# Two channels to a weight load in the last four table builds of a fused linear-attention and state-space kernel

## The chip, the cores and the metric

The kernel runs on one core of one Trainium2 chip. The metric is the device time of one execution in microseconds. The core has five engines that run side by side and wait for each other by semaphores: TensorE (PE, matmuls, and PEld, its weight loads), VectorE (DVE), ScalarE (ACT), GpSimd (POOL) and SyncE (SP). SP, POOL and ACT also issue DMAs, each in the order of its own queue. Matmul results land in PSUM and are copied out ("evicted") by ACT or DVE.

## The reference

Two independent parts share one output of 2048 rows and 896 columns.

Part A is a linear attention with 16 heads of 28 channels. Queries and keys go through a 28x28 matrix per head and become features by softmax of the plus and of the minus value; the output is `phi_q (phi_k^T v) / (phi_q sum(phi_k) + 1e-6)`, followed by the output projection.

Part B is a long convolution over 2048 positions for each of 448 channels. Its kernel is a sum over 256 complex states:

```python
P = jnp.exp(logdA[:, :, None] * l[None, None, :])
K = jnp.einsum("dn,dnl,dn->dl", Cc, P, dB).real
...
Yf = Uf * Kf[None, :, :, :]
```

with `logdA = dt * (A_re + i A_im)`. The convolution is done by Fourier transform in the reference; `u * Dskip` is added.

## The kernel before, in words

**Part B's table.** The position l is split into a high part (32 values, list `HI`) and a low part (50 values, list `LO`). For each state, `exp(logdA * l)` is the product of a high power, times C and B, and a low power. So K for one channel is a 32 x 50 table: the matrix product of the high rows (tile `U`, 256 states x 32) with the low rows (tile `W`, 256 states x 50), over real and imaginary parts. The 448 channels are done in eight groups k = 0 to 7 of 56 channels. The 256 states are two halves of 128, which lie on the partitions.

For each group there are five steps:
- `dampings` (L687) makes the damping factors by Exp on ACT, `rotations` (L692) the cosines and sines by Sin on ACT, both out of PSUM.
- `hi_tables` (L714) makes the high rows from powers of the step: four levels with a product of 1792 elements and then sums, differences or the pair step, and two levels (the fourth and the sixth) in which a DMA on POOL's queue adds to what is there. A copy of the first four rows comes by DMA, and two small copies with signs (`SN`) by ACT or DVE.
- `damp` (L700) multiplies rotations by dampings on DVE in two products (step damp) and negates a part on ACT or DVE (step neg, L712).
- `build_k` (L761) forms the tables: in two halves of seven channels from each of four quarters, 112 matmuls a half, each with a weight load of 32 columns (one channel's high rows) and 50 moving columns (its low rows). Channels of the four quarters use the four 32-column strips of the array side by side; four matmuls accumulate (two state halves, real and imaginary). Each half is evicted, 350 columns, into `Ts`.
- `scatter_k` (L903) moves the tables by many small DMAs into `Kt`, ordered by position. It exists once for groups 0 to 3 (sc0), once for 4 and 5 (sc1), once for 6 and 7 (sc2), 48 DMAs each.

Then `kernel_spectrum` (steps ks0, ks1, ks2) multiplies `Kt` with Fourier tables on PE, `signal_spectrum` (us) does the same for the signal, `conv_group` (conv0 to conv2) multiplies the two spectra on DVE, `inverse` (inv) goes back on PE, and the result is written. The products of conv2 need the tables of groups 6 and 7.

**Part A** is woven in: `key_pair` (key, kn), `query` (qe, qz, q), with Exp on ACT, products at L878 and L349 on DVE.

**Order.** Each operation is recorded as a unit by a helper (`tt` L349, `act` L362, `copy` L372, `mm` L382, `dma` L397), and nothing is issued at once. The list `ORDER` names every unit with its engine (P, V, A, G, S for PE, DVE, ACT, POOL, SP), and `PLACES` names the PSUM buffer kind of each PSUM tile. `Plan.run` issues the units in this order; each engine works through its own part of the list and stops at the first instruction whose inputs are not there. Both lists were written by a planner outside the kernel. Some units may go to either ACT or DVE (evictions, sign copies, negations); the list decides.

Of the kernel before, what the change touches and what calls it, by code (L numbers as in the profile page):

```python
# [9 lines left out]
BF16 = mybir.dt.bfloat16  # L10
# [53 lines left out]
def _dft_tables():  # L64
# [27 lines left out]
    for hh in range(4):  # L92
# [3 lines left out]
ORDER = ("23G 26P 39P 0A 48A 29P 24P 3S 1S 2S 4S 17G 8G 34P 27P 44P 43P 13S 192S 47P 49V 52V 51V 53V 50V 54P 55V 56P 57A "  # L96
# [200 lines left out]
def kernel(  # L297
# [134 lines left out]
    Wr = sb("W", [128, 2, N_LO, 2, COLS], BF16, oW)  # L432
    W = Wr.rearrange("p k l c x -> p k c l x")
    E = sb("E", [128, 2, N_LO - 1, COLS], BF16, oE)
    U = sb("U", [128, 2, N_HI, 2, COLS], BF16, oU)
    Kt = sb("Kt", [128, N_KT, D_MODEL], BF16, 0)


# [721 lines left out]
```

## Time and profile before

| | |
|---|---|
| median of 3 runs | 290.28 us (289.6 to 291.36) |
| the profiled execution | 289.75 us |
| its span, first to last instruction | 287.9 us |
| mean granted TensorE clock | 0.992 |
| PE, PEld busy | 253.1, 202.6 us |
| DVE busy | 268.4 us (360 instructions) |
| ACT busy | 239.3 us (537 instructions) |
| POOL busy | 82.8 us |

Times in the profile are microseconds from the start of the span. A group of instructions is given with its line, engine, operation, shapes and count, then the busy time and the mean duration in ns, then the time the engine was idle just before them and what ended that. Instructions on one engine overlap a little, so durations are longer than the distance from start to start. Helpers give their line to all that is recorded through them: L349 are all products and sums on DVE, L362 the functions on ACT, L372 evictions, L382 matmuls, L397 DMAs.

### The profile page before, as it was taken

The page shows a single profiled execution, that of the slowest core. Times are in us where ns is not written, and L with a number is a line of the kernel's source. Part 1 is how long each engine was busy: PE and PEld are TensorE (multiplying, and loading weights), DVE is VectorE, ACT ScalarE, POOL GpSimd, SP SyncE. Part 2 cuts the span into 40 slices and gives each one's busy share as a digit, 9 for nine tenths or more (in the row PEclk, how much of TensorE's full clock was granted, in tenths as well). Part 3 has the DMA queues.
Part 4 walks back from the last instruction along what each step waited for, and adds up shares of the span by engine and source line. Part 5 has one row for each costly group of instructions (what it writes and reads, how often), then busy time and mean ns, then how long its engine had stood idle before and what let it go on. Part 6 is the DMA issues. An engine that isn't in the chain of part 4 may idle for free.

```text
span 287.9 us, 10151 instructions
## 1 busy us (share of the span) xinstructions
PE 253.1 (88%) x4280; PEld 202.6 (70%) x4280; DVE 268.4 (93%) x360; ACT 239.3 (83%) x537; POOL 82.8 (29%) x133
## 2 busy tenths in 40 slices
PE   7895798989978989979888889999899798999993
PEld 3454347668944778957755777769889687989983
DVE  2999997999999999999999999999999989799990
ACT  2999989999999999999999999999996162473241
POOL 2011024050604002030198232468250299000000
PEclk9999899999999999999999999999999999999999
DMA  6996333181546115142064255269969669786033
GB/s 186 298 268 179 71 96 82 24 207 27 84 81 138 32 29 107 34 100 61 11 116 70 56 113 141 54 112 293 238 137 287 224 163 242 222 270 227 18 128 130
DMA packets 41678, 38.54 MB, mean 134 GB/s; under 512 B 21168, under 2 KB 39000, under 8 KB 41506
## 3 DMA queue, kind: packets, MB, share of 16 engines
q1 hardware_dynamic: 33701, 30.14, 36.2%
q0 software_dynamic: 6480, 7.72, 14.9%
q8 instruction: 33, 0.54, 0.8%
q10 hardware_dynamic: 1453, 0.05, 0.3%
q14 instruction: 11, 0.09, 0.1%
HBM read 23.99 MB, written 7.34 MB: 109 GB/s over the span
## 4 chain that ended last, share of the span: by engine, by line
ACT 38%; DVE 23%; PE 14%; DMA 13%; issue 8%; SPq 2%; ACTq 1%; POOL 0%; DVEq 0%; POOLq 0%
ACT sbuf L362 29%; DVE sbuf L349 19%; PE mm L382 7%; ACT sbuf L372 6%; DMA sbuf<-sbuf 5%; PE kb L382 4%; DMA SUd<-sbuf 3%; SPq L397 2%; ACT L362 2%; DVE sbuf L372 2%; PE arg L382 2%; DMA sbuf<-in_B_u_dram 2%; DMA sbuf<-SUd 2%; DMA sbuf<-in_B_A_re_dram 1%; DVE sbuf L353 1%
## 5 line engine op out<-in xcount | busy, mean ns | idle before, releaser
L382 PEld LDWEIGHTS <-sbuf 128*32 128x32 bf16 (+4 forms) x4056 | 190.5, 119 | 72.5 <-issue 39.1
L349 DVE TENSOR_TENSOR sbuf<-sbuf 128x448 bf16<-128x448 bf16 (+9 forms) x213 | 205.3, 1007 | 2.6 <-ACT sbuf L372 1.8
L382 PE MATMUL mm<-sbuf 128*32 128x50 bf16 (+9 forms) x2676 | 157.0, 262 | 18.7 <-ACT sbuf L372 11.1
L362 ACT ACTIVATE sbuf<-arg 128x224 bf16<-128x224 f32 (+5 forms) x312 | 136.8, 676 | 0.1
L397 POOL DMA_DIRECT2D sbuf<-sbuf x99 | 65.0, 762 | 106.5 <-DVE sbuf L349 44.7
L372 ACT CAST sbuf<-mm 128x448 bf16<-128x448 f32 (+3 forms) x90 | 56.5, 657 | 21.5 <-PE mm L382 19.7
L382 PE MATMUL kb<-sbuf 128*32 128x50 bf16 (+10 forms) x790 | 64.6, 250 | 5.6 <-issue 2.0
L382 PE MATMUL arg<-sbuf 128*128 128x112 bf16 (+4 forms) x590 | 44.6, 225 | 1.4 <-ACT sbuf L362 1.2
L372 ACT CAST sbuf<-kb 128x448 bf16<-128x448 f32 (+4 forms) x42 | 24.2, 611 | 12.7 <-PE kb L382 11.0
L397 POOL DMA_DIRECT2D SUd<-sbuf x18 | 14.3, 827 | 45.4 <-ACT sbuf L372 35.9
L362 ACT ACTIVATE sbuf<-mm 112x512 bf16<-112x512 f32 x38 | 24.9, 798 | 0.0
L878 DVE TENSOR_TENSOR sbuf<-arg,sbuf 128x896 bf16<-128x896 f32 x16 | 17.3, 1085 | 1.3 <-PE kb L382 0.6
L362 ACT ACTIVATE sbuf<-sbuf 128x896 f32<-128x896 f32 (+3 forms) x13 | 13.0, 1038 | 1.8 <-DMA sbuf<-in_B_log_dt_dram 1.8
L362 ACT ACT_TABLE_LOAD x10 | 12.8, 1283 | 1.4 <-PEq L1144 1.2
L372 DVE CAST sbuf<-mm 128x448 bf16<-128x448 f32 (+2 forms) x17 | 10.1, 592 | 0.4 <-PE mm L382 0.3
L349 DVE TENSOR_TENSOR sbuf<-mm,sbuf 128x896 bf16<-128x896 bf16 (+1 forms) x17 | 9.3, 554 | 0.0
L812 PE MATMUL mm<-sbuf 112*128 112x112 bf16 x112 | 7.8, 212 | 1.7 <-DVE sbuf L807 0.9
L812 PEld LDWEIGHTS <-sbuf 112*128 112x128 bf16 x128 | 7.3, 97 | 2.7 <-issue 2.4
L372 DVE COPY sbuf<-kb 112x512 bf16<-112x512 bf16 (+1 forms) x18 | 7.2, 406 | 1.5 <-PE kb L584 1.5
L584 PEld LDWEIGHTS <-sbuf 128*112 128x112 bf16 x64 | 5.3, 129 | 3.9 <-issue 3.0
L584 PE MATMUL kb<-sbuf 128*112 128x128 bf16 x64 | 6.1, 219 | 2.2 <-DVE sbuf L372 1.3
L372 ACT CAST sbuf<-arg 128x224 bf16<-128x224 f32 (+1 forms) x10 | 3.5, 373 | 5.0 <-PE arg L382 5.0
(39 smaller groups left out, 69.9 us busy)
## 6 DMA issues: line engine op xcount, KB each, us to landing
sbuf<-const SPq DMA_DIRECT2D x37, 224.0 KB
sbuf<-sbuf POOLq DMA_DIRECT2D x21, 224.0 KB, 4.1
sbuf<-const SPq DMA_DIRECT2D x6, 512.0 KB
sbuf<-in_B_u_dram SPq DMA_DIRECT2D x6, 448.0 KB
sbuf<-in_A_x_dram SPq DMA_DIRECT2D x4, 448.0 KB
out_dram<-sbuf SPq DMA_DIRECT2D x16, 112.0 KB
sbuf<-SUd SPq DMA_DIRECT2D x1, 1792.0 KB
sbuf<-SUd SPq DMA_DIRECT2D x2, 896.0 KB
```

Source lines behind the costliest of these rows:

```text
L349: lambda: nc.vector.tensor_tensor(out=at(out_), in0=at(a), in1=at(b), op=op), [whose(a), whose(b)], [out_])
L353: lambda: nc.vector.scalar_tensor_tensor(out=at(out_), in0=at(a), scalar=sc, in1=at(b), op0=op0, op1=op1),
L362: lambda: nc.scalar.activation(at(out_), at(a), func, scale=scale, bias=bias),
L372: lambda e: (nc.scalar.copy if e == "ACT" else nc.vector.tensor_copy)(at(out_), at(a)), [whose(a)], [out_])
L382: nc.tensor.matmul(out_, lhsT=lhsT, rhs=rhs, start=start, stop=stop, **kw)
L397: plan.add({e: own[e] for e in engs}, lambda e=engs[0]: QUEUES[e].dma_start(out=out_, in_=in_, **kw), r, w, lat=lat, load=pieces / 16000 * ...
L584: mms(p, [lambda t, j=j, x=x: nc.tensor.transpose(t[:, j, :], x[:, 112 * j:112 * j + 112], ident[:, :]) for j in range(4)], 0.4, [x, ident ...
L812: mms(pt, [lambda t, i=i, s=s, c=c: nc.tensor.transpose(t[:, s, 112 * c:112 * c + 112], EKT[:, s, c, 128 * i:128 * i + 128], id112) for s ...
L878: nc.vector.tensor_tensor(out=heads, in0=num(pn.t), op=ALU.mult, in1=SC[:, t4].unsqueeze(3).to_broadcast([128, 2, 16, D_HEAD]))
```

## The change

- In groups 4 to 7 the build takes two channels at once: a weight load of 64 columns (the high rows of two channels) and 100 moving columns (the low rows of both). Of the four 32 x 50 products that come out, the two in which both sides are of the same channel are used. Two such matmuls lie side by side in the two 64-column halves of the array. A group takes 112 matmuls instead of 224, in three PSUM tiles of 5, 5 and 4 channel columns (40, 40 and 32 matmuls), evicted with 500, 500 and 400 columns.
- For that the high rows are kept as two halves of 56 columns (`US`), and `hi_split` takes the place of `hi_tables` in these groups: each product of 1792 elements becomes two of 896, the pair step's two operations become four, the first copy two DMAs.
- `Ts` of groups 4 to 7 holds both columns of products, so it is twice as large and lies elsewhere; `scatter_k` reads the half that belongs to a channel. The order of channels within the states changes for all groups (`states`).
- `ORDER` and `PLACES` are new throughout: 1601 units instead of 1565.

```diff
-        return t.rearrange("p (c n g q) -> p n c g q", c=NCHK, n=2, g=4)
+        return t.rearrange("p (c g n q) -> p n c g q", c=NCHK, n=2, g=4)
...
+    def hi_split(k, rank):
+        step(f"hi{k}.0", rank)
+        cols = slice(k * COLS, (k + 1) * COLS)
+        u = US[:, k % 2]
...
+        for v in range(2):
+            dma(["SP", "POOL"], u[:, v, 0:4].rearrange("p n r x -> p (n r) x"), split(H[:, :, :, cols])[:, v],
+                r=[H[:, :, :, cols]], w=[u[:, v, 0:4]])
+
+        def times(j, src):
+
+            t2 = sb("t2", [128, 2, 2, 4, 2, CW], BF16, oT2)
+            for i in range(2):
...
+                tt(t2[:, i], a, power(j, i).unsqueeze(2).to_broadcast([128, 2, 8, CW]), ALU.mult)
+            return t2
...
+                dma(["POOL"], dst, t2[:, :, :, :, :], r=[t2[:, :, :, :, :], dst], w=[dst], lat=6, cost=0.85, accum_op=ALU.add)
...
+                for v in range(2):
+                    tt(pair(v, 9, 15), a[:, v, ::-1], b[:, v], ALU.subtract)
+                    tt(pair(v, 8, 17), a[:, v], b[:, v, ::-1], ALU.add)
...
-    def build_k(k, Ts, x0, rank):
-        for hq in range(2):
-            step(f"build{k}.{hq}", rank)
+    def build(k, Ts, x0, rank):
+        wide = k > 3
+        for part, (q0, nq) in enumerate(((0, 5), (5, 5), (10, 4)) if wide else ((0, 7), (7, 7))):
+            step(f"build{k}.{part}", rank)
             p = ps(("mm", "kb"), [128, 512])
             calls = []
-            for qq in range(7):
-                q = 7 * hq + qq
+            for qq in range(nq):
                 for i in range(4):
                     nch, ri = i // 2, i % 2
-                    for g in range(4):
-                        xc = nch * CW + g * NQ + q
-                        calls.append(lambda t, g=g, qq=qq, i=i, ri=ri, xc=xc: mm(
-                            t[32 * g:32 * g + 32, qq * N_LO:(qq + 1) * N_LO], U[:, k % 2, :, ri, xc],
-                            W[:, k % 2, ri, :, xc], i == 0, i == 3, tile_position=(0, 32 * g)))
...
+                    for g in range(2):
+                        xc = 28 * g + NQ * nch + q0 + qq
+                        if wide:
+                            calls.append(lambda t, g=g, qq=qq, i=i, ri=ri, xc=xc: mm(
+                                t[64 * g:64 * g + 64, qq * 2 * N_LO:(qq + 1) * 2 * N_LO].rearrange("p (v l) -> p v l", v=2),
+                                US[:, k % 2, :, :, ri, xc].rearrange("p v h -> p (v h)"),
+                                W[:, k % 2, ri, :, xc:xc + CW + 1:CW].rearrange("p l v -> p v l"),
+                                i == 0, i == 3, tile_position=(0, 64 * g)))
+                            continue
...
+            if wide:
+                copy(Ts[:, :, :, x0 + q0:x0 + q0 + nq],
+                     (p, lambda t, nq=nq: t[:, 0:2 * N_LO * nq].rearrange("p (c v l) -> p v l c", c=nq, v=2)))
...
-                    v = Ts[32 * g + h0:32 * g + h1, l0:l1:s, :]
+                    p1 = 64 * (g % 2) + 32 * (g // 2)
+                    v = (Ts[:, g // 2] if gi else Ts)[p1 + h0:p1 + h1, l0:l1:s, :]
...
-        hi_tables(k, 1020 + 100 * k)
+        (hi_split if k > 3 else hi_tables)(k, 1020 + 100 * k)
```

More of the change, by code (lines that the diff above doesn't have):

```diff
@@ L94, in _dft_tables @@
     return tuple(_round_bf16(t) for t in (G, GI, FT, pid, hm))
-ORDER = ("23G 26P 39P 0A 48A 29P 24P 3S 1S 2S 4S 17G 8G 34P 27P 44P 43P 13S 192S 47P 49V 52V 51V 53V 50V 54P 55V 56P 57A "
[75 rows of a table removed]
-PLACES = ("kmmkmmmmkmkmmkmkkmmkmkkmmkmkmkmmmammkkmkkmkmkmkmkkkkmkmmkmkkmmmmkkkmmkmmkaakkmmakakmmkmakkmkmkmkmmkmmkmmmmamaamm"
-         "ammmammmmmmmmmmmmmmmamammammmmmmmmamamaamammmmammmmammmmmmammammmmmmmmmmkamkakaamkkammkakakkmkmmakmakammkkmkmamk"
-         "kammkmkmkkmammkmkkaammakmkmkmkkmamkmkamkmaammkmmkkmmamkmakmmkmmkkmmaammmakmkmkmmma")
+ORDER = ("17G 23G 33P 35P 42P 27P 31P 0A 48A 44P 26P 40P 34P 2S 1S 6S 49V 50V 53V 51V 52V 56P 57V 54P 84P 85V 55A 67A 3S "
[77 rows of a table added]
+PLACES = ("kmmkkkkkmmmkkmmkkkkmkmkmkmkkmmkkkmmmkkmmkmkamkmkmkkmkkmkkkmkmmkkmmkmkmkmkmkkammamkakmmkmakmmkmmkmmmkkmmammamamma"
+         "mmmmammmmmmmmmmmmammammmammammmmmammmmaamammammmmmmmmammmaammammmmmamkkkamkmaakamakkmmkmkaakmmakkmmmmkaakmkmkakk"
+         "kmmmmakkkamkkmmmkkmamkaakmmkmkkmakmkmamkkkmmmakmkakmmmkkakmkmmakmkammkmamammkmaakmmmkk")
 ENGINES = {"P": "PE", "V": "DVE", "A": "ACT", "G": "POOL", "S": "SP"}
@@ L406 @@
     SN = sb("SN", [128, 2, COLS], BF16, oPID + 3584)
+    SNS = sb("SNS", [128, 2, 2, CW], BF16, oPID + 3584)
     H = sb("H", [128, 4, 2, NCOL], BF16, oH)
@@ L435 @@
     U = sb("U", [128, 2, N_HI, 2, COLS], BF16, oU)
+    US = sb("US", [128, 2, 2, N_HI, 2, CW], BF16, oU)
     Kt = sb("Kt", [128, N_KT, D_MODEL], BF16, 0)
@@ L759, in hi_tables, with split, power, pair @@
                 tt(dst[:, :, 1], t2[:, 0, :, 1], t2[:, 1, :, 0], ALU.add)
-    def build_k(k, Ts, x0, rank):
-        for hq in range(2):
-            step(f"build{k}.{hq}", rank)
+    def hi_split(k, rank):
+        step(f"hi{k}.0", rank)
+        cols = slice(k * COLS, (k + 1) * COLS)
+        u = US[:, k % 2]
+        def split(t):
+            return t.rearrange("p n r (v x) -> p v (n r) x", v=2)
+        def power(j, i):
+            return PW[j][:, i, cols].rearrange("p (v x) -> p v x", v=2)
+        for v in range(2):
[4 more added lines that the diff above has]
+            for i in range(2):
+                if src is H:
+                    a = split(src[:, :, :, cols])
+                else:
+                    a = src.rearrange("p v n r x -> p v n (r x)")
+                tt(t2[:, i], a, power(j, i).unsqueeze(2).to_broadcast([128, 2, 8, CW]), ALU.mult)
+            return t2
+        step(f"sn{k}", rank)
+        sine = power(512, 1)
+        for r, f in enumerate((1.0, -1.0)):
+            plan.add({"ACT": 0.15, "DVE": 0.11}, lambda e, r=r, f=f: nc.scalar.mul(SNS[:, :, r, :], sine, f) if e == "ACT" else
+                     nc.vector.tensor_scalar_mul(SNS[:, :, r, :], sine, f), [sine], [SNS[:, :, r, :]])
+        for lv, (j, dst, src, tmp) in enumerate(((256, u[:, :, 8:12], H, None), (128, None, u[:, :, 8:12], None),
+                                                 (512, u[:, :, 16:20], u[:, :, 0:16:4], None),
+                                                 (512, u[:, :, 20:24], u[:, :, 2:16:4], 3584),
+                                                 (512, u[:, :, 24:28], u[:, :, 16:20], None),
+                                                 (512, u[:, :, 28:32], u[:, :, 24:28], 5376))):
+            step(f"hi{k}.{lv + 1}", rank)
+            if tmp:
+                t2 = sb("tm", [128, 2, 4, 2, CW], BF16, oT2 + tmp)
+                tt(t2[:, :, :, ::-1, :], src.rearrange("p v n r x -> p v n (r x)"),
+                   SNS.rearrange("p v r x -> p v (r x)").unsqueeze(2).to_broadcast([128, 2, 4, COLS]), ALU.mult)
+                tt(dst, src.rearrange("p v n r x -> p v n (r x)"),
+                   power(512, 0).unsqueeze(2).to_broadcast([128, 2, 8, CW]), ALU.mult)
+                dma(["POOL"], dst, t2[:, :, :, :, :], r=[t2[:, :, :, :, :], dst], w=[dst], lat=6, cost=0.85, accum_op=ALU.add)
+                continue
+            t2 = times(j, src)
+            if dst is None:
+                uf = u.rearrange("p v n r x -> p v (n r) x")
+                a, b = (t2[:, i].rearrange("p v n r x -> p v r n x") for i in range(2))
+                def pair(v, first, gap):
+                    w = uf[:, v, first:first + gap + 7]
+                    return bass.AP(tensor=w.tensor, offset=w.offset, ap=[w.ap[0], [gap * CW, 2], [2 * CW, 4], [1, CW]])
+                for v in range(2):
+                    tt(pair(v, 9, 15), a[:, v, ::-1], b[:, v], ALU.subtract)
+                    tt(pair(v, 8, 17), a[:, v], b[:, v, ::-1], ALU.add)
+                tt(uf[:, :, 8:16], uf[:, :, 8:16],
+                   BACK[:, cols].rearrange("p (v x) -> p v x", v=2).unsqueeze(2).to_broadcast([128, 2, 8, CW]), ALU.mult)
+            else:
+                tt(dst[:, :, :, 0], t2[:, 0, :, :, 0], t2[:, 1, :, :, 1], ALU.subtract)
+                tt(dst[:, :, :, 1], t2[:, 0, :, :, 1], t2[:, 1, :, :, 0], ALU.add)
@@ L775, in build_k @@
-            mms(p, calls, 2.9, [U[:, k % 2], W[:, k % 2]], mode=1, act=4800)
-            copy(Ts[:, :, x0 + 7 * hq:x0 + 7 * hq + 7],
-                  (p, lambda t: t[:, 0:7 * N_LO].rearrange("p (c l) -> p l c", c=7)))
+                    for g in range(2):
[6 more added lines that the diff above has]
+                                i == 0, i == 3, tile_position=(0, 64 * g)))
+                            continue
+                        for v in range(2):
+                            calls.append(lambda t, g=g, qq=qq, i=i, ri=ri, xc=xc, v=v: mm(
+                                t[64 * g + 32 * v:64 * g + 32 * v + 32, qq * N_LO:(qq + 1) * N_LO], U[:, k % 2, :, ri, CW * v + xc],
+                                W[:, k % 2, ri, :, CW * v + xc], i == 0, i == 3, tile_position=(0, 64 * g + 32 * v)))
@@ new lines, in build @@
+            mms(p, calls, 0.0265 * len(calls) if wide else 2.9, [U[:, k % 2], W[:, k % 2]], mode=1,
+                act=100 * len(calls) if wide else 4800)
+            if wide:
+                copy(Ts[:, :, :, x0 + q0:x0 + q0 + nq],
+                     (p, lambda t, nq=nq: t[:, 0:2 * N_LO * nq].rearrange("p (c v l) -> p v l c", c=nq, v=2)))
+            else:
+                copy(Ts[:, :, x0 + q0:x0 + q0 + nq],
+                     (p, lambda t: t[:, 0:7 * N_LO].rearrange("p (c l) -> p l c", c=7)))
@@ L1067, in table @@
         gi = (0, 0, 0, 0, 1, 1, 2, 2)[k]
-        if k in (0, 4, 6):
-            tss[gi] = sb("Ts", [128, N_LO, 28 * GROUPS[gi][1]], BF16, oTs + (2744 if gi == 2 else 0))
+        if k == 0:
+            tss[0] = sb("Ts", [128, N_LO, 56], BF16, oTs)
+        elif k in (4, 6):
+            tss[gi] = sb("Ts", [128, 2, N_LO, 28], BF16, (oV - 96, oTs)[gi - 1])
         damp(k, 1000 + 100 * k)
-        build_k(k, tss[gi], NQ * (k - (0, 4, 6)[gi]), 1000 + 100 * k)
+        build(k, tss[gi], NQ * (k - (0, 4, 6)[gi]), 1000 + 100 * k)
     def chunk(k, exps, rots):
```

152 rows, old and new, of the table ORDER are left out of this document.

## The prediction

> **What bounds the kernel now.** I read the busy time and the 40 slices first, then the busy time of each engine in single stretches, then the groups by shape, the chain that ended last, and the timeline of DVE.
>
> ```profile
> PE 253.1 (88%) x4280; PEld 202.6 (70%) x4280; DVE 268.4 (93%) x360; ACT 239.3 (83%) x537; POOL 82.8 (29%) x133
> DVE  2999997999999999999999999999999989799990
> ACT  2999989999999999999999999999996162473241
> ...
> 160.00:185.00 25.00, 22.60 (x609) 19.08 (x608) 24.66 (x37) 24.97 (x61) 7.20 (x11) 1.00 0.41 96
> 213.00:233.00 20.00, 17.46 (x384) 15.49 (x382) 19.37 (x13) 10.95 (x22) 4.55 (x9) 1.00 0.77 238
> 251.00:280.00 29.00, 27.86 (x463) 26.67 (x461) 28.23 (x28) 12.90 (x31) 0.00 (x0) 1.00 0.50 163
> ```
>
> A stretch shows its length, then busy us (and instructions) of PE, PEld, DVE, ACT, POOL. Up to 213 us DVE and ACT are both full: 24.66 and 24.97 of 25 us. From 213 us ACT has room (10.95 of 20), and DVE stays near full to 280 us (28.23 of the last 29). PE is never the fullest engine before 213 us, though its share (22.6 of 25) includes waits inside pipelined matmuls. So two engines bound the first three quarters, and DVE, fed by PE, the last.
>
> ```profile
> L382 PE MATMUL mm<-sbuf 128*32 128x50 bf16 x1568 | 38.7, 269 | 2.5 <-issue 2.0 <-ACT sbuf L372 0.4
> L349 DVE TENSOR_TENSOR sbuf<-sbuf 128x1792 bf16<-128x1792 bf16 x47 | 50.2, 1077 | 0.0
> L349 DVE TENSOR_TENSOR sbuf<-sbuf 128x448 bf16<-128x448 bf16 x48 | 16.6, 377 | 0.0
> L372 ACT CAST sbuf<-mm 128x350 bf16<-128x350 f32 x9 | 6.3, 704 | 2.1 <-PE mm L382 2.1
> L712 ACT ACTIVATE sbuf<-sbuf 128x1680 bf16<-128x1680 bf16 x4 | 7.2, 1803 | 0.0
> ...
> 125.63 0.38 DVE L349 TENSOR_TENSOR sbuf<-sbuf 128x448 bf16<-128x448 bf16 x1
> 125.93 0.61 DVE L372 CAST sbuf<-mm 128x448 bf16<-128x448 f32 x1
> 126.46 1.08 DVE L349 TENSOR_TENSOR sbuf<-sbuf 128x1792 bf16<-128x1792 bf16 x1
> 127.46 0.61 DVE L349 TENSOR_TENSOR sbuf<-mm,sbuf 128x896 bf16<-128x896 bf16 x1
> 128.00 0.61 DVE L349 TENSOR_TENSOR sbuf<-sbuf 128x896 bf16<-128x896 bf16 x1
> ```
>
> The build matmuls take 38.7/1568 = 24.7 ns of PE each, so one group (224) some 5.5 us. On a full engine an instruction costs its start-to-start time, not its duration: the timeline gives 1.00 us for 1792 elements, 0.54 for 896, 0.30 for 448, and 0.53 for an eviction of 448. On ACT, back-to-back starts give 0.42 us for a 448-column eviction, 0.48 for 512, 0.36 for the strided 350, 1.50 for the negation at L712, 0.14 for 112 columns.
>
> ```profile
> 215.30 4.11 DVE L349 TENSOR_TENSOR sbuf<-sbuf 128x7616 bf16<-128x7616 bf16 x1
> 279.88 0.61 DVE L349 TENSOR_TENSOR sbuf<-sbuf 128x896 bf16<-128x896 bf16 x1
> ...
> 220.41 2.67 PE mm L382 x100
> 223.09 1.28 PE kb L382 x51
> 224.37 1.95 issue
> 226.32 1.51 PE kb L382 x49
> ```
>
> The end hangs on group 7: its damping (damp7) leaves DVE at 219.3, its build runs on PE from 220.4 to 227.8 with a gap of 1.95, then come eviction, scatter, the last spectra and the last DVE product, done at 280.5. DVE works nearly all of those 61.2 us: its instructions there sum to 57.5 by starts, which leaves 3.7 us of waits.
>
> **Builds, PE.** 896 pairs of 32-column load and 50-column matmul (896 x 24.7 ns = 22.1 us) become 448 pairs of 64 and 100. No row shows such a pair. Lower bound: the same 24.7 ns, as if each pair cost its issue alone; upper bound: the untiled 128x112 matmul, 20.8 us/380 = 54.7 ns, scaled to 100 columns, 49 ns. The tiled builds are the nearer row; I take 28 ns, 12.5 us. PE is relieved of 9.6 us (bounds 0.1 and 11.0), 2.4 us a group. For groups 4 to 6 the time is hidden behind full DVE and ACT and counts nothing; if that cover were gone it would be up to 7.2 us. For group 7 it shortens the build in the chain, but DVE has other work meanwhile: nothing again.
> The row says a 50-column matmul costs about 25 ns. [...]
>
> **High rows, DVE.** Per group hi_split cuts each of the four products of 1792 into two of 896 (+4 x 0.08 us) and the pair step from two of 896 to four of 448 (+0.13): some +0.4 us, +1.6 us for four groups. Rows are 56 elements instead of 112 now. If short rows lost the bf16 rate, 896 elements would take the 1.0 us of f32 operands instead of 0.54, some +20 us over four groups; but the key product at 127.46 steps through rows of four at 0.54, which excludes that end. I take zero, also for the runs of 14 that the new layout of the states gives to the first evictions: these read f32 from PSUM at 0.53 for 448 either way. Each group's first copy becomes two DMAs (four more, 0.76 us on POOL or 0.4 on SP; they start early, so nothing).
>
> **Evictions.** A wide group evicts 500+500+400 columns instead of 2 x 350. On ACT 500 lies between 448 and 512: 0.47 us; 400: 0.38. The other end is the 350's excess over its count (0.36 against 0.34) scaled up: 0.50, which is 0.2 us for all.
>
> **What the new lists move.** I counted the instructions ahead of group 7's last damping in both lists, because there both full engines have to be through.
> - DVE, +1.25 us: products +1.6; seven sign copies fewer (-0.7); two negations more (+1.07); evictions (three of 350 fewer, one of 500 and three of 448 more, two of 448 in halves and four small ones fewer) -1.4; one 896-wide product from PSUM in f32 more and one in bf16 fewer (+0.47); reciprocals and small ones +0.2.
> - ACT, up to the last rotation of group 7, +1.7 us: four evictions of 500, two of 400, two of 350 fewer, +1.9; seven sign copies +1.0; two negations fewer -3.0; other evictions (four of spectra that now come earlier, three of weight folds taken over from DVE, one of 512, less four of 448) +1.8. Table loads stay at ten.
>
> Both were full, so one or the other is owed: I take +1.5, ends +1.2 and +1.7 (less 1.3 if the longest DVE wait between 40 and 60 us, for a transpose, went too).
> - Start: the first input in SP's queue is now A_re, on which the first transposes waited; dt still has to pass ACT and DVE until 5.4, PE began at 5.8. At most -0.4; I take 0.
> - POOL issues 18 DMAs more, SP 13 fewer. At 0.76 us POOL carries 14 us more, against 205 us in which it is not busy. The accumulating DMAs of the high rows stand in that queue between scatters, so a scatter that waits for an eviction holds them back; see the rivals.
> - Behind damp7, DVE has the same 57 us. PE has 2.4 us of build less, but two kernel-spectrum pieces (ten 224-column matmuls each, 1.9 us) and pieces of three query tiles (some 2.9 us) more: +2.4 against about 4 us in which it stood open. Ends: -3.7 (all DVE waits there close) and +2.4; I take 0, because DVE's sum is unchanged.
>
> Sum against the profiled execution: span 287.9 + 1.5 = 289.4; the execution took 289.75, 1.85 more than its span, so 291.3. The median of the three runs lies 0.53 above that execution: 291.8 us.
>
> **Rivals.**
> 1. Faster. With PE looser the new list closes the DVE waits behind damp7: evictions and spectra arrive on time. For it: the longest of them, 1.75 us ahead of a 3584-element product at 251.5, was for an ACT eviction of a spectrum. Against it: DVE and ACT before that owe 1.5. It gives 1.5 - 3.7 = -2.2, thus 288.1; with the early wait gone too, 286.8. It decides once more than 3 us of those waits close.
> 2. Slower by POOL. The accumulations of groups 6 and 7 (two of the six levels) stand in POOL's queue between scatters of groups 4 and 5, which wait for builds to be evicted; one such scatter stood ahead of group 7's last accumulation after its predecessor, now five do. Its input was ready at 210 and the build began at 220.4; if it is held until the build waits, that build, its scatter and all behind are late by a queue of five scatters, 5 x 0.76 = 3.8 us: 295.6. It decides once the 10 us between are used up, by the add's own 4.1 us to landing (the page's DMA issues) and the queue.
> 3. The change saves PE nothing: at 49 ns the last build takes 5.5 us as before, and PE has 4.8 us more behind damp7, against 4 us in which it stood open. If all of the open time can be used, 0.8 is left; if none, 4.8; I take the middle, +2.8: 294.6. It decides from about 40 ns a pair. [...]
>
> **How the numbers follow.** 0.5% of 290.3 is 1.45 us, about what a measurement here can tell from no change. Forecast (both full engines owe their added work) 0.42, own range 290.5 to 293.5; rival 1 0.34; rival 2 0.13; rival 3 0.11. Forecast splits into 0.27 slower and 0.15 same, rival 1 into 0.31 faster and 0.03 same, the other two are slower. So faster 0.31, same 0.18, slower 0.51. The range leaves 1 in 10 on either side: from 286.8, the far end of rival 1, to 295.6, rival 2.
>
> **What would show it.** Right: build matmuls of 100 columns at 25 to 30 ns in the groups by shape; DVE and ACT full up to the last rotation, which ends at 215 to 216 us instead of 213.9; damp7 off DVE at 220 to 221; DVE busy about 270 us and PE near 243. Wrong: the last rotation at or before 213.9 (the order took idle time that I did not see), DVE waits behind damp7 under 1.5 us (rival 1), POOL waits ahead of a build (rival 2), build matmuls above 40 ns (rival 3).

## The result, and the profile after

The changed kernel takes 313.64 us (median of 4 runs, 313.02 to 314.19) against 289.94 us before in the same comparison: a ratio of 1.082, 95% interval 1.075 to 1.089. The forecast of 291.8 us and its range (to 295.6) missed by far. The profiled execution took 313.62 us, its span is 311.8 us.

Line numbers shift with the change: in the profiles of after, L384 are matmuls, L351 products on DVE, L364 functions on ACT, L374 evictions, L956 the query's product.

Busy times and two of the 40-slice rows of after:

```profile
PE 273.5 (88%) x3832; PEld 222.4 (71%) x3832; DVE 271.3 (87%) x378; ACT 242.6 (78%) x547; POOL 97.3 (31%) x151
...
DVE  3899999999999999599998496789957389999992
ACT  4989999999999999988999494799965156444411
```

PE issues 448 matmuls fewer and is busy 20.4 us longer (253.1 before; the forecast was 243). DVE and ACT have about the work that was forecast, but where both were full before, DVE has a hole in slice 16 (of 0 to 39; 125 us) and both have many from slice 22 on (172 us).

The groups by shape show where PE's time is (busy us, then mean ns of one):

```profile
L384 PE MATMUL kb<-sbuf 128*64 128x100 bf16 x232 | 21.5, 356 | 0.8 <-DVE sbuf L351 0.7
L384 PE MATMUL mm<-sbuf 128*32 128x50 bf16 x896 | 21.3, 269 | 2.3 <-DVE sbuf L351 2.3
L384 PE MATMUL mm<-sbuf 128*64 128x100 bf16 x216 | 20.2, 357 | 0.0
```

The 896 narrow matmuls left in groups 0 to 3 take 21.3 us. The 448 wide ones of groups 4 to 7 take 41.7 us, 93 ns each, where 28 were forecast. From start to start a wide pair takes 88.6 ns and a group 9.9 us. The timeline of PE over group 4's build, and of DVE in the wait behind group 7's damping:

```profile
167.78 6.64 PE L384 MATMUL mm<-sbuf 128*64 128x100 bf16 x72
174.24 3.74 PE L384 MATMUL kb<-sbuf 128*64 128x100 bf16 x40
...
240.45 3.89 DVE L351 TENSOR_TENSOR sbuf<-sbuf 128x7168 bf16<-128x7168 bf16 x1 [0.68 <-ACT sbuf L374]
250.73 1.09 DVE L956 TENSOR_TENSOR sbuf<-arg,sbuf 128x896 bf16<-128x896 f32 x1 [6.38 <-PE arg L384]
```

DVE waits 6.38 us for a query matmul that stands behind the build in PE's order. The list of waits (total us, times, longest) has this as DVE's largest, and beside it a wait that the kernel before didn't have:

```profile
DVE sbuf L956 <- PE arg L384: 15.9, 5, 6.4
DVE sbuf L351 <- DMA sbuf<-sbuf: 6.3, 2, 3.2
```

Busy time by stretch (length, then PE, PEld, DVE, ACT, POOL):

```profile
160.00:185.00 25.00, 21.72 (x270) 19.39 (x270) 19.67 (x31) 20.21 (x46) 9.75 (x15) 0.93 0.41 79
185.00:213.00 28.00, 25.41 (x249) 19.89 (x247) 22.31 (x36) 21.56 (x51) 17.11 (x26) 1.00 0.51 100
233.00:251.00 18.00, 18.00 (x213) 16.91 (x210) 9.39 (x5) 6.56 (x11) 0.15 (x1) 1.00 0.53 173
```

In the first of these DVE and ACT had 24.66 and 24.97 of 25 us before; now both have a fifth of it open. Start of the last operation of a step, in us from the start of the span:

| step | before | after |
|---|---|---|
| damping of group 4 | 147.7 | 147.8 |
| rotations of group 5 | 170.9 | 179.4 |
| damping of group 6 | 194.8 | 209.6 |
| rotations of group 7 | 213.3 | 229.6 |
| damping of group 7 | 215.3 | 233.0 |
| last eviction of build 7 | 227.9 | 249.8 |
| last product of conv2 | 279.9 | 303.9 |

Up to the first wide build, at 167.8 us, at most 2 us are lost (ACT's table load at 162.9 comes at 164.9; the hole in slice 16 is the first of the two DMA waits). Then every wide build leaves some microseconds behind: 17.7 us by the last damping, 24 at the end.

### The profile page after: what moved, and what is told of

Its sections match the earlier page's. It is cut to its first block, busy times and chain, and to the rows that moved or that the text cites. A ratio compares the mean times of both kernels' runs of the same rounds, so it can differ in the third digit from the quotient of the medians.

```text
span 311.8 us, 9289 instructions
## 1 busy us (share of the span) xinstructions
PE 273.5 (88%) x3832; PEld 222.4 (71%) x3832; DVE 271.3 (87%) x378; ACT 242.6 (78%) x547; POOL 97.3 (31%) x151
## 5 line engine op out<-in xcount | busy, mean ns | idle before, releaser
L384 PEld LDWEIGHTS <-sbuf 128*128 128x128 bf16 (+5 forms) x3608 | 210.0, 124 | 75.4 <-issue 41.9
L351 DVE TENSOR_TENSOR sbuf<-sbuf 128x896 bf16<-128x896 bf16 (+9 forms) x237 | 208.1, 925 | 7.9 <-DMA sbuf<-sbuf 6.3
L384 PE MATMUL mm<-sbuf 128*32 128x50 bf16 (+10 forms) x2108 | 150.7, 270 | 17.2 <-ACT sbuf L374 10.6
L364 ACT ACTIVATE sbuf<-arg 128x224 bf16<-128x224 f32 (+5 forms) x314 | 135.8, 671 | 0.1
L399 POOL DMA_DIRECT2D sbuf<-sbuf x111 | 75.5, 868 | 110.5 <-DVE sbuf L351 58.8
L384 PE MATMUL kb<-sbuf 128*64 128x100 bf16 (+10 forms) x918 | 86.0, 266 | 8.7 <-DVE sbuf L351 3.0
L374 ACT CAST sbuf<-mm 128x448 bf16<-128x448 f32 (+5 forms) x89 | 56.5, 661 | 35.0 <-PE mm L384 27.9
L384 PE MATMUL arg<-sbuf 128*128 128x112 bf16 (+3 forms) x582 | 47.9, 233 | 3.5 <-ACT sbuf L364 2.1
L374 ACT CAST sbuf<-kb 128x448 bf16<-128x448 f32 (+4 forms) x45 | 28.7, 653 | 23.8 <-PE kb L384 19.1
L956 DVE TENSOR_TENSOR sbuf<-arg,sbuf 128x896 bf16<-128x896 f32 x16 | 17.3, 1090 | 18.3 <-PE arg L384 15.9
L364 ACT ACTIVATE sbuf<-mm 112x512 bf16<-112x512 f32 x32 | 20.3, 769 | 0.0
L364 ACT ACTIVATE sbuf<-sbuf 128x896 f32<-128x896 f32 (+3 forms) x13 | 12.7, 1016 | 1.7 <-DMA sbuf<-in_B_log_dt_dram 1.7
L374 DVE CAST sbuf<-mm 128x448 bf16<-128x448 f32 (+2 forms) x15 | 9.2, 613 | 1.1 <-issue 1.1
L351 DVE TENSOR_TENSOR sbuf<-mm,sbuf 128x896 bf16<-128x896 bf16 (+1 forms) x15 | 8.6, 576 | 0.2 <-PE mm L890 0.2
L374 DVE COPY sbuf<-kb 112x512 bf16<-112x512 bf16 (+2 forms) x17 | 7.0, 427 | 1.5 <-PE kb L597 1.3
L364 ACT ACTIVATE sbuf<-kb 112x512 bf16<-112x512 f32 x14 | 8.0, 650 | 0.0
L368 ACT CAST sbuf<-sbuf 128x1792 bf16<-128x1792 f32 (+1 forms) x5 | 7.4, 1484 | 0.0
```

The costliest lines, as they stand in the source:

```text
L351: lambda: nc.vector.tensor_tensor(out=at(out_), in0=at(a), in1=at(b), op=op), [whose(a), whose(b)], [out_])
L364: lambda: nc.scalar.activation(at(out_), at(a), func, scale=scale, bias=bias),
L368: plan.add({"ACT": 0.09 + count(out_) * 0.833e-3}, lambda: nc.scalar.copy(at(out_), at(a)), [whose(a)], [out_])
L374: lambda e: (nc.scalar.copy if e == "ACT" else nc.vector.tensor_copy)(at(out_), at(a)), [whose(a)], [out_])
L384: nc.tensor.matmul(out_, lhsT=lhsT, rhs=rhs, start=start, stop=stop, **kw)
L399: plan.add({e: own[e] for e in engs}, lambda e=engs[0]: QUEUES[e].dma_start(out=out_, in_=in_, **kw), r, w, lat=lat, load=pieces / 16000 * ...
```

## The experiments

In these diffs `lhs` and `rhs` are the weights and the moving columns of a pair. "Burst" numbers are distances from start to start, the mean over one build.

**Narrow builds in the new list, and a quarter of the wide ones.** First: is it the wide pair, or the list?

```diff
 # e1_narrow: the two channels one by one, four strips, evictions of the same size
+                            for v in range(2):
...
+                                    t[64 * g + 32 * v:64 * g + 32 * v + 32, qq * N_LO:(qq + 1) * N_LO],
+                                    US[:, k % 2, v, :, ri, xc], W[:, k % 2, ri, :, CW * v + xc],
 # e2_quarter: only the first of the four products that accumulate
+                            if i:
+                                continue
```

> Undoes one part of the change: in groups 4 to 7 the builds are again pairs of 32 weight columns and 50 moving columns, one channel each (896 pairs), out of the new high rows, in the same units, the same order lists and three PSUM tiles a group; the evictions keep their 500, 500 and 400 columns (the 250 or 200 that are there are read twice). Theory A, the time went to the price of the wide pair (41.7 us for 448 in the profile after, 93 ns each, against the 28 ns that were assumed): PE gets some 20 us back, and the time comes to 290 to 294 us. Theory B, the new order lists or the high rows cost a good part of it: it stays above 300 us.

> Takes the price away: of the four wide matmuls that accumulate for a pair of channels only the first is left (one state half, real part), so 28 pairs a group instead of 112; the other three products are left out and the output lacks them. At 89 ns a pair that is 2.5 us a group, near the 3.1 us that the prediction had assumed for all 112. Theory A: this is the time that the prediction was about, 291.8 us if its sum held, 287 to 288 us if its rival 1 (DVE waits close) did. Theory B: it stays above 298 us.

The narrow builds: 300.13 us, ratio 1.033 (1.030 to 1.037), 23 to 23.6 ns a pair. The quarter of the wide builds, 2.5 us a group, the cost that the forecast had given a whole build: 293.29 us, ratio 1.011 (1.006 to 1.017). So 13.5 of the 23.7 us go with the wide pair against the narrow one, and 20.4 with builds as cheap as forecast. Some 10 us against before remain with narrow pairs, and the new list, the new high rows and the larger evictions share them: the new kernel wants builds of about 3 us, and narrow ones of 5.2 us, with which the old list runs its 290 us, cost it some 7 us.

With a quarter of the pairs DVE's waits are down to two kinds worth naming:

```profile
DVE sbuf L351 <- DMA sbuf<-sbuf: 6.3, 2, 3.2
DVE sbuf L360 <- ACT sbuf L364: 4.3, 1, 4.3
```

The second was there before (4.5 us, at the start). The first is taken up below.

**What sets the price of a pair.** The high rows of a channel lie 112 elements apart (224 bytes), its low rows 224 elements apart (448 bytes). The next kernel makes one side or both contiguous in single groups, which gives wrong tables there; the one after changes the columns and the order of the strips.

```diff
 # e3_strides
+                            if k in (4, 6):
+                                lhs = US[:, k % 2].rearrange("p v h r x -> p (v h r x)")[:, 64 * xc:64 * xc + 64]
+                            if k in (5, 6):
+                                rhs = Wr[:, k % 2].rearrange("p l c x -> p (l c x)")[:, 100 * xc:100 * xc + 100]...
 # e4_widths: group 4 64 weights and 50 moving columns, group 5 32 and 100 on four strips, groups 6
 # (64 and 100) and 7 (32 and 50) all of one strip, then all of the next
+                calls = [c for _, c in (sorted(calls, key=lambda z: z[0]) if k > 5 else calls)]
```

> The wide pair with other addresses, one form a group, so that the tables of groups 4 to 6 are not the right ones: group 4 loads 64 weight columns that lie side by side (the kernel's lie 112 elements apart), group 5 moves 100 columns that lie side by side (the kernel's lie 224 elements apart), group 6 does both, group 7 is as in the kernel. Theory S, the stride makes the pair slow: below 88 ns, some 55 ns in group 5 if it is the moving side, some 65 ns in group 4 if it is the weights, 35 ns in group 6. Theory T, load and matmul follow each other in one strip of the array and each column costs some 1.08 ns wherever it lies: 88 ns in all four groups.

> The price taken apart by size and by strip, one form a group. Group 4: 64 weight columns, 50 moving, two strips (the second channel's column of the table is left out). Group 5: 32 weight columns, 100 moving, four strips, 224 pairs. Group 6: 64 and 100 as in the kernel, but all pairs of one strip first, then all of the other. Group 7: 32 and 50, four strips, one strip after the other. Theory T (in one strip a pair takes 1.08 ns times the sum of weight and moving columns, strips run side by side): 61, 36, 177 and 90 ns a pair. Theory S, moving columns alone at 1.77 ns, strips side by side: 44, 44, 177 and 88. Theory U, pairs are bound by one common path that all strips share, not by their own strip: groups 6 and 7 keep 89 and 23 ns.

In e4_widths group 4 forms only half of its tables. The two kernels took 307.39 and 330.13 us (one run each); bursts in ns a pair:

| pair | weights | moving | strips | ns a pair | ns x strips |
|---|---|---|---|---|---|
| 64 and 100 (control) | strided | strided | 2 | 89.2 | 178 |
| 64 and 100 | contiguous | strided | 2 | 85.2 | 170 |
| 64 and 100 | strided | contiguous | 2 | 58.7 | 117 |
| 64 and 100 | contiguous | contiguous | 2 | 22.2 | 44 |
| 64 and 50 | strided | strided | 2 | 60.3 | 121 |
| 32 and 100 | strided | strided | 4 | 45.3 | 181 |
| 32 and 50 (groups 0 to 3) | strided | strided | 4 | 22.7 | 91 |
| 64 and 100, strips one by one | strided | strided | one at a time | 150 | |
| 32 and 50, strips one by one | strided | strided | one at a time | 72.4 | |

The last column reads simply: 1.8 ns for each strided column, by whichever of weights (64: 117 and 121) and moving columns (100: 170 to 181; 50: 91) has more. The strips do this side by side. The theory that a pair costs the sum whatever its stride, 88 ns in all three groups of the first kernel, falls; the stride theory has the mechanism, but its numbers (55, 65, 35) took the two sides as a sum, and they go side by side. In the second kernel the strips one by one rose to 150 and 72 ns, so interleaved strips do share the time. These two are means over pairs that overlap wherever one strip gives way to the next; inside a strip the starts lie 172 and 87 ns apart (medians), so one strip alone shows the 1.7 ns a column.

The timeline of the first kernel over two bursts of 40 pairs in group 6, and, in an ordinary pair of rows, group 7's control:

```profile
220.48 1.07 PE L384 MATMUL kb<-sbuf 128*64 128x100 bf16 x40
223.61 1.07 PE L384 MATMUL kb<-sbuf 128*64 128x100 bf16 x40 [2.06 <-DVE sbuf L351]
...
233.36 3.09 PE L384 MATMUL mm<-sbuf 128*64 128x100 bf16 x32 [0.36 <-ACT sbuf L374]
236.24 7.37 PE L384 MATMUL kb<-sbuf 128*64 128x100 bf16 x80
```

40 contiguous pairs take 1.07 us, 80 strided ones 7.37.

**All pairs, contiguous; and the new DMA wait.** Here every wide pair but the first two of a PSUM tile reads contiguous elements, then the second DMA of the first high-row copy is moved in the list.

```diff
 # e5_contig
+                            if qq or i:
+                                j = 2 * xc + ri
+                                lhs = US[:, k % 2].rearrange("p v h r x -> p (v h r x)")[:, 64 * j:64 * j + 64]
+                                rhs = Wr[:, k % 2].rearrange("p l c x -> p (l c x)")[:, 100 * j:100 * j + 100]...
 # e6_copies (with e5_contig), in ORDER; group 4, then group 6
-"... 782G ... 791V ... 783G 790V ... 1083S ... 1084G ..."
+"... 782G 783G ... 791V ... 790V ... 1083S 1084S ..."
 # e9_copies_later (with e5_contig)
+"... 782G ... 791V ... 790V ... 796V 783G ... 1083S 1084S ..."
 # e11_after_copies: the changed kernel itself, with the same places as e9_copies_later
```

> The changed kernel with all 112 pairs of 64 and 100 columns a group, but with contiguous operands: except for the first two pairs of each PSUM tile, which keep theirs so that the build waits for the same inputs, a pair reads 64 adjacent elements of the high rows and 100 adjacent elements of the low rows, spread over the whole of both tiles. The tables are then wrong; count, shapes, accumulation, evictions and lists stay. Theory A (the price of a pair is set by reading its operands in strides: 64 or 100 columns at 1.8 ns in each strip): 22 to 24 ns a pair, 2.9 us a group with the first pairs, no DVE wait for the key and query products, and a median of 293 to 295 us, as with a quarter of the pairs. Theory B (112 pairs that overlap with other work on PE cost more than their own time, by sequencer, weight loads or PSUM): 297 to 302 us although a pair is cheap.

> The same, and in the order list the second DMA of the first copy of groups 4 and 6 is issued right behind the first one (in group 6 on SP's queue as the first), instead of between the two products of the next level but one. If the two DVE waits of 3.2 us for a DMA are owed to these two DMAs and lie on the path: they go, and the time falls by 4 to 6 us against the contiguous build, to 287 to 290 us. If they are hidden, as other waits would take their place: less than 1 us. If the waits are for another DMA: they stay.

> The contiguous builds again, and the second DMA of group 4's first copy moved the other way, behind the pair step and its scaling, ahead of the next product that reads its rows; in group 6 as in the run before. Theory: the waits of DVE are no need of the computation. The two halves of the high rows lie one behind the other in one tile, so an operation on rows 8 to 11 of both halves spans rows 0 to 3 of the second half, which this DMA writes, and is made to wait for it. Then the wait of 4.8 us in group 4 goes and the time falls by another 2 to 4 us, to 288 to 289.5 us; the terms of DVE (+1.25) and ACT (+1.7) then stand against a DVE that has no waits left but the one at the start. If the wait only moves to the product that does read these rows: 291 to 292 us.

> The changed kernel with its own wide builds and the two DMAs placed as in the first of these runs. If the two waits of 3.2 us lie on the path although the builds bind behind them: 307 to 310 us. If a late build takes their place: 312 to 314 us.

| kernel | median, us | ratio to before | 95% interval |
|---|---|---|---|
| e5_contig | 293.30 | 1.016 | 1.009 to 1.024 |
| e6_copies | 291.65 | 1.007 | 1.003 to 1.012 |
| e9_copies_later | 289.40 | 0.996 | 0.993 to 0.999 |
| e11_after_copies | 310.92 | 1.070 | 1.064 to 1.076 |

With the operands contiguous a group takes 112 x 27.6 ns = 3.1 us, and the time is that of the quarter of the pairs: theory A. Between e11_after_copies and e9_copies_later the operands' addresses alone differ, and 21.5 us lie between them, for 4 x (9.9 - 3.1) = 27 us of PE.

With the DMA moved up, the wait in group 6 went, but the one in group 4 came earlier and grew:

```profile
130.67 0.69 DVE L351 TENSOR_TENSOR sbuf<-sbuf 128x448 bf16<-128x448 bf16 x2 [4.81 <-DMA sbuf<-sbuf]
```

It now stood ahead of the sums that write rows 8 to 11, not only of a product that reads them. The copy itself can't start before build 2 has left that buffer (its last matmul ends at 125.2 here, and the DMA starts at 125.24). With group 4's DMA behind the pair step both waits are gone, and e9's list of DVE waits begins (here L340 are products, L353 functions, L363 evictions):

```profile
DVE sbuf L349 <- ACT sbuf L353: 4.5, 1, 4.5
DVE sbuf L363 <- PE kb L586: 1.5, 1, 1.5
DVE sbuf L340 <- ACT sbuf L353: 1.0, 2, 0.7
```

That agrees with an operation over both halves being made to wait for a DMA into rows between them. The operations were not split by halves, so this cause is supported by where the wait went, not isolated. Its price: 3.9 us with cheap builds (293.30 to 289.40), some 2.7 us in the changed kernel, where the intervals of the two ratios touch.

**The same dose in the old list.**

```diff
 # e7_before_cheap
+                    if k > 3 and i:
+                        continue
 # e8_before_dear
+                    for again in range(1 + (k > 3)):
...
-                            W[:, k % 2, ri, :, xc], i == 0, i == 3, tile_position=(0, 32 * g)))
+                                W[:, k % 2, ri, :, xc], i == 0 and not again, i == 3 and again == (k > 3), ...
```

> The kernel before with only the first of the four accumulating matmuls in the builds of groups 4 to 7 (56 pairs of 32 and 50 a group instead of 224; the other three products are left out): PE has some 4.1 us less a group. It asks what a cheap build would be worth in the old list. If DVE and ACT bound it and the build is hidden: within 1 us of the time before, 290 to 291. If PE's builds bind behind the last damping (the waits of DVE there, 3.7 us in all): 287 to 289.

> The kernel before with each matmul of the builds of groups 4 to 7 issued twice in a row (448 pairs of 32 and 50 a group; these tables come out doubled): 11 us a group, near the 9.9 us of the wide pairs. It asks whether the loss hangs on the time that a build takes on PE alone, whatever the list. If every list passes it on as the new one does (13.5 of 18.8 us): some 16 us more, 305 to 308 us. If the old list has room on PE: less than 8 us more, 294 to 298 us, and then the new list is at fault too.

Cheap builds: 291.19 us, ratio 1.006 (1.002 to 1.010). Dear ones: 316.16 us, ratio 1.094 (1.087 to 1.101), some 26 us for about 21 us of PE, more than the 16 expected. With cheap builds DVE and ACT are nearly as full as before up to 213 us (the second stretch before, then both of e7_before_cheap):

```profile
185.00:213.00 28.00, 26.98 (x482) 22.44 (x481) 27.57 (x44) 27.94 (x65) 18.52 (x30) 1.00 0.78 188
...
160.00:185.00 25.00, 16.50 (x272) 12.89 (x270) 24.75 (x37) 24.97 (x62) 7.00 (x11) 0.82 0.40 92
185.00:213.00 28.00, 24.28 (x304) 18.73 (x303) 27.30 (x43) 27.07 (x63) 17.84 (x30) 0.87 0.74 183
```

With dear ones they have the holes of the changed kernel (the same of e8_before_dear):

```profile
160.00:185.00 25.00, 22.08 (x681) 19.54 (x683) 18.22 (x26) 19.00 (x42) 5.94 (x8) 1.00 0.39 85
185.00:213.00 28.00, 27.72 (x571) 22.82 (x560) 23.22 (x33) 23.74 (x57) 14.06 (x23) 1.00 0.48 125
```

So a loss of this size doesn't need the new list: the old one passes a build of 11 us on in full. And in the old list a build of some 1.3 us gained nothing on balance: with it the kernel is even 0.6% slower than before. The balance has two parts. From group 7's damping to the end of the span it takes 70.1 us against 72.6, so behind the damping a cheap build was worth 2.5 us. But that damping begins at 218.57 instead of 215.30, as DVE waits for a query's product just ahead of it, at the end of a stretch with half the granted clock:

```profile
206.70:216.90 10.20, 7.55 (x62) 5.49 (x63) 8.04 (x15) 9.17 (x25) 4.22 (x6) 0.50 0.74 170
...
217.56 1.09 DVE L880 TENSOR_TENSOR sbuf<-arg,sbuf 128x896 bf16<-128x896 f32 x1 [2.06 <-PE arg L382]
```

Ten spectrum matmuls of 224 columns took 2.02 us there, 1.13 before. The mean granted clock was 0.934 to 0.941 in all eight executions of this kernel, and 0.968 to 1.000 in those of the kernel before beside them. The rows point to the clock, but no run had the cheap builds at a full clock, so what they would be worth then stays open.

**How far apart columns may lie.** Two more kernels for prices alone (307.25 and 300.11 us, one run each): the step between columns on both sides, and narrow pairs with one side or both contiguous.

```diff
 # e10_steps (group 7: narrow pairs, both sides contiguous); e12_lines has {4: 4, 5: 6}, and narrow pairs
 # with contiguous moving columns (group 6) or contiguous weights (group 7)
+                                s, j = {4: 2, 5: 8, 6: 32}[k], 2 * xc + ri
+                                lhs = US[:, k % 2].rearrange("p v h r x -> p (v h r x)")[:, 32 * j:32 * j + 64 * s][:, ::s]
```

> One look at prices: pairs of 64 and 100 whose operands are read with a step of 2 elements (group 4), 8 (group 5), 32 (group 6), both sides alike, the first two pairs of each tile left as they are; group 7 pairs of 32 and 50 on four strips with contiguous operands. Tables of these groups are wrong. If any step but one makes the slow read: 88 ns in groups 4 to 6. If the read goes by blocks of bytes: few columns share a block at step 2, so about 25 to 45 ns there, more at 8, 88 at 32. For group 7: below 20 ns if the strided read alone held the narrow pair at 22.5 ns; 22 ns if that is also the least distance from start to start.

> Prices again. Groups 4 and 5: pairs of 64 and 100 read with a step of 4 elements (8 bytes) and of 6 (12 bytes) on both sides, the first two pairs of each tile left as they are. Groups 6 and 7: pairs of 32 and 50 on four strips, group 6 with the weights in their strided place and contiguous moving columns, group 7 the other way round. Tables of these groups are wrong. A step of 2 elements cost 24 ns and one of 8 some 89. [...] If the price grows with the bytes stepped over: near 45 at step 4 and 65 at step 6. For the narrow pairs, one strip reads 1.8 ns a strided column, weights and moving columns side by side, and four strips work at once: 32 x 1.8 / 4 = 14 ns in group 6, 50 x 1.8 / 4 = 22.5 ns in group 7. If weights and moving columns of a strip are read one after the other, group 6 and group 7 fall by the same share each and neither stays at 22.5.

Distance between two pairs of one strip, the median of the starts inside a burst; the last two columns are worked out, the time by each of the 100 columns, and that by each byte of the step:

| step, bytes | ns a strip | ns a column | ns a column and byte |
|---|---|---|---|
| 2 (e5_contig) | 46 | 0.46 | 0.23 |
| 4 | 49 | 0.49 | 0.12 |
| 8 | 94 | 0.94 | 0.12 |
| 12 | 138 | 1.38 | 0.12 |
| 16 | 183 | 1.83 | 0.11 |
| 64 | 170 | 1.70 | 0.03 |
| 448 (moving), 224 (weights), after | 176 | 1.76 | |

From 4 to 16 bytes the price grows with the step, 0.11 to 0.12 ns a column for each byte, and at 64 and 448 bytes it is no higher than at 16 (170 and 176 ns against 183). From 4 bytes to 2 it falls only from 49 to 46 ns. So steps are not slow alike: 49 ns at 4 bytes against 183 at 16. A read by blocks of bytes, the other case in the expectation for e10_steps, agrees with these rows, but no run shows the blocks themselves.

The narrow pairs: 8.1 ns with both sides contiguous, 15 to 16 with the weights strided (18.5 over the first two tiles with the pause between them), 21 to 22 with the moving columns strided. The timeline of the first of these, over one tile of 64 and another of 76 pairs:

```profile
235.14 0.68 PE L384 MATMUL mm<-sbuf 128*32 128x50 bf16 x64
235.63 0.82 PE L384 MATMUL kb<-sbuf 128*32 128x50 bf16 x76
```

140 narrow pairs end 1.3 us after the first starts; 112 of them took 2.74 us before. The expected 14 and 22.5 ns came out nearly.

## Why the prediction was wrong

**The step that failed** is "Builds, PE": "The tiled builds are the nearer row; I take 28 ns", with bounds of 24.7 and 49 ns. Measured: 88.6 ns from start to start, 93 ns of busy time. The 24.7 ns of a narrow pair were read as the cost of issuing one. They are a quarter of the time in which four strips each read 50 strided columns (91 ns). The wide pair doubles the columns of a strip and halves the number of strips, so a pair costs four times as much and a group twice, 9.9 us instead of 5.2. The upper bound was taken from an untiled matmul with another layout, so it bounded nothing. The trace of before could have shown it: inside a build there, four starts lie within 25 to 35 ns, then comes a pause of some 50 to 65 ns, and the next four follow (medians of six of the eight builds). Evenly spaced starts would have spoken for issue; bunches of four speak for four strips that are each busy for some 90 ns. The addresses stood in the diff, with steps of `CW` and of a whole row.

**"As if each pair cost its issue alone"**, the lower bound. No run shows 24.7 ns to be that cost: narrow pairs on four strips start every 8.1 ns once they are contiguous (e10_steps, group 7). Nor was it weighed that the operands are read in strides: a wide pair takes 88.6 ns with the kernel's addresses and 22.2 ns with contiguous ones (e3_strides, group 6).

**"For groups 4 to 6 the time is hidden behind full DVE and ACT and counts nothing."** Up to 213 us DVE and ACT do stay nearly full in the old list with a shorter build (e7_before_cheap, at a lower clock). The step failed for a longer one, to which it was carried over only as a remark of "up to 7.2 us". In after, the matmuls of queries and of the next arguments stand behind the build in PE's order, and DVE and ACT run dry: +8 us by group 5's rotations, +15 by group 6's damping, +18 by group 7's. The reading that PE is never the fullest engine before 213 us isn't so in the first 10 us of before, where PE is busy 8.23 us and DVE 4.38; no term hangs on it.

**Rival 3** (PE saves nothing) had the mechanism at the wrong size: it ended at 49 ns and 294.6 us, and counted only what lies behind the last damping. PE's cost goes through from the first wide build on.

**"The first copy two DMAs ... they start early, so nothing."** Wrong by 2.7 us. The first starts early; the second was placed ahead of products that then wait for it (in group 4 between two of them), 6.3 us in two waits here, 6.3 to 8.0 in each run of the new list that kept its place.

**DVE +1.25 and ACT +1.7, the forecast's sum.** DVE's busy time was forecast near 270 and is 270.2 to 271.5 in all runs of the new list. With a cheap pair and without the DMA wait (e9_copies_later) group 7's damping begins at 216.26 against 215.30, 0.96 late: DVE's term, near enough. The high rows keep their rate (98 products of 896 elements, 618 ns each, as the 0.61 us before). The eviction of 500 columns was taken at 0.47 us; those followed by other work took 0.56 to 0.66, 0.1 to 0.2 us more each. "Last rotation at 215 to 216" and "damp7 off DVE at 220 to 221" failed in after (229.6 at its start, and 237), mostly by the builds: that damping begins at 233.0 in after, at 221.6 with contiguous operands (e5_contig) and at 216.3 without the DMA waits as well.

**Behind damp7: "I take 0", and rival 1.** "For group 7 ... nothing again" doesn't hold for a cheap build: already in the old list it takes 2.5 us less behind that damping (e7_before_cheap). In e9_copies_later the stretch from that damping to the end of the span is 69.9 us against 72.6 before: 2.7 of the 3.7 us of waits close, once the pair is cheap. So rival 1's mechanism was in the list. That profiled execution was the fastest of ten (287.94 us, median 289.40), so its two differences, together 1.7 us faster, overstate the gain; by the medians the list more than paid for the rest, by 0.4%, at most 0.75%. But there the pairs read the wrong elements; a layout in which the right ones lie side by side was not made, and what writing the rows so would cost is open.

**Rival 2** (POOL's queue) did not come. PE's waits in after hold 0.5 us for a DMA within SBUF, although POOL has 14.5 us more to do, as forecast.

## What to carry to other kernels

The time of a tiled matmul divided by the number of strips was no issue cost here (24.7 ns, and 8.1 with contiguous operands): look at the starts within a burst, and price one strip by itself before changing how many there are. A matmul's operands should be priced by their addresses as well as by their columns: 64 and 100 of them took 88.6 or 22.2 ns here. And before costing a saving on an engine, ask what it is worth in the kernel at all: a quarter of the pairs in the old list gave 291.19 us and showed no gain, and twice the pairs how much there was to lose.

## What the runs showed of the hardware

- In e3_strides, e4_widths, e10_steps and after, operands of a tiled matmul with columns 16 bytes or more apart cost 1.7 to 1.9 ns a column in each strip, weights and moving columns side by side, so the larger of the two counts; contiguous ones cost 0.44 to 0.46 ns in pairs of 64 and 100 (e3_strides, e5_contig), and about 0.65 (4 x 8.1 ns for 50) in pairs of 32 and 50 (e10_steps). A pair of 64 and 100 falls from 88.6 (after) to 22.2 ns, one of 32 and 50 from 22.7 (groups 0 to 3 of after) to 8.1.
- In these traces the strided price doesn't follow the granted clock, the contiguous one does. In group 6 of e3_strides a burst of 32 contiguous pairs at a clock of 0.50 took 40.5 ns a pair against 22.2 at 1.00; narrow contiguous ones (e10_steps, group 7) took 10.2 ns a pair in the 84 from 238.97 us, in a slice whose clock lies between 0.7 and 0.8, against 8.1 at 1.00. Strided pairs strip by strip (e4_widths) start 172 ns apart inside a strip up to 227.8 us, at 1.00, and from there to the end of the tile, at 0.50; all starts counted, 65 pairs take 9.0 us at a mean clock of 0.77 (138 ns each), and 28 take 4.0 us at 0.50 (143 ns). The rows for the pairs of e3_strides, with the clock in the third column from the right:

```profile
220.80:221.50 0.70, 0.70 (x35) 0.63 (x29) 0.70 (x3) 0.70 (x3) 0.70 (x3) 1.00 0.59 136
...
226.90:228.20 1.30, 1.30 (x33) 1.18 (x30) 1.30 (x2) 1.11 (x3) 1.30 (x4) 0.50 1.10 191
```
